# A third set of exponentials, and a head's transposes and output one slot later, evenly spread

## The chip, the cores and the metric

The kernel runs on one core of a Trainium2 chip. The metric is the device time in microseconds (us), the median over several runs; lower is better. The engines that the text speaks of are TensorE (PE; PEld is its weight loads), VectorE (DVE), ScalarE (ACT), GpSimd (POOL), and SyncE (SP), which issues most of the DMAs.

## The reference

Block-causal attention over 8 batches of 8 heads, and a bilinear feed-forward layer on its output, all in float32:

```python
# q, k, v: (8, 8, 576, 64); w_a, w_b: (512, 1536); w_out: (1536, 512)
scores = q @ k.transpose(0, 1, 3, 2) / sqrt(64)
scores = where(pos_q // 64 >= pos_k // 64, scores, -1e9)
attn = exp(scores - max(scores)); attn = attn / (sum(attn) + 1e-9)
x = (attn @ v).transpose(0, 2, 1, 3).reshape(4608, 512)
out = ((x @ w_a) * (x @ w_b)) @ w_out
```

## The kernel before, in words

The 64 heads are worked through in **slots**, one head's scores per slot (the loop at L599). Three generators hold a head's steps, and a table of steps, `SLOT` (L595), says in which order a slot runs them, for which head, and with how many filling matmuls behind each.

- `softmax(i)` (L374), in slot i: on PE the scores, in five groups, named here by their width: the side block (L412, 128 columns) with the last tile `sl` (512, L392), then 256, 320 and 448 columns. Each has its maximum on DVE (L398) and its exponentials on ACT (L401, written into the tiles `e` and `e_s`). The last step comes at the start of slot i+1: row sums and reciprocals on DVE (L435 to L442, `rc`), then POOL multiplies all the tiles of exponentials by them (L445). Score tiles come from a ring of three PSUM banks (`ps_sc`, L262), and a head uses four; the side block and the 320 columns share one.
- `turn(i)` (L450): PE transposes the exponentials in four groups (L468), here T3, T2, T1 and T0 after the tile that they read (T1 has `e_s` as well). Each goes to one of two PSUM buffers called `tp`; ACT rounds it to `ah` (L470) and DVE takes the remainder `al` (L472, in `lower`). `SLOT` runs T3, T2 and T1 of head s-1 late in slot s, and T0 early in slot s+1. `lower` of T1 is issued only with the next step, and those of T1 and T0 are put behind the reciprocals `rc` of the next head (`behind_of`).
- `values(i)` (L484), in slot i+2: the output in two steps, here V1 (four matmuls with `ah`, L517) and V2 (the side block and four with `al`, L521 and L523), into the one PSUM bank `av` and one more `tp` buffer. ACT and DVE add it up into `xf` (L527 to L532); after every second head it is split into `xh` and `xl` and stored.

The exponentials live in `NE` = 2 sets of buffers (L283), taken in turn, so head i+2 writes where head i was read. Heads 0 to 7 (`NATIVE`) run in plain float32, without `al`.

From slot 10.2 on (`MOE_FROM`) PE gets filling work: the feed-forward layer of the batches that are done (`first_pass`, L545, matmuls of 288 columns at L217, called the filling matmuls below). `want` (L583) says how many of them have been issued at a given point of a slot: an even ramp up to 240 at slot 2·8+`LAG`, then 36 to a slot (one for each unit of the third number in `SLOT`). Every second slot also prepares queries and keys of two heads (L337 to L345) and issues the DMAs that spread them (L356 to L359); `split_v` (L361) prepares the values of the head before. Weights are converted meanwhile, mostly on DVE (`convert`, L127). After the last slot come the rest of the first pass and two further passes, whose code the change does not touch.

Each engine's instructions are put into one fixed order when the program is built, and each engine then works in that order. "Head 44 is of batch 5, number 4" is how the names in the built order are read: `tp_2_0` is T0 of number 2 of its batch; the last number of a name is that of the buffer.

Of the kernel before, what the change touches and what calls it, by code (L numbers as in the profile page):

```python
# [26 lines left out]
MOE_FROM = 10.2  # L27
# [4 lines left out]
XQ = lambda nc: nc.scalar  # L32
PE_ORDER = []
NATIVE = 8
SPARE = 8
WARM = 9
KEEP = {(0,3):4,(1,0):2,(1,1):2,(1,2):2,(1,3):6}
# [15 lines left out]
def attention_then_bilinear_ffn(  # L53
# [10 lines left out]
    nc = tc.nc  # L64
    B, H, D, S = kT.shape
# [39 lines left out]
    def f32(ap):  # L105
        return ap.bitcast(F32)

    def split(hi, lo, src, hi_eng, lo_eng):
        if hi_eng is nc.scalar:
            nc.scalar.copy(hi, src)  # L110
        else:
            hi_eng.tensor_copy(hi, src)
        return lo_eng.tensor_tensor(lo, src, f32(hi), op=ALU.subtract)  # L113
# [3 lines left out]
    def behind_of(ins, key):  # L117
        if key in last:
            tc.add_manual_dep(ins.ins, last[key].ins.name, NOSYNC, reason="after work that is waited for")
# [88 lines left out]
    marks = []  # L208
# [71 lines left out]
    W = S - BLK  # L280
    SIDE, SIDE_T = 3, 1
    SC = slice(P * SIDE_T, P * SIDE_T + BLK), slice(P * SIDE_T + BLK, P * (SIDE_T + 1))
    NE = 2  # L283
    e_bufs, s_bufs = [], []
    for i in range(NE):
        es = [const.tile([P, ew[t]], F32, name=f"e{i}_{t}") for t in range(NT)]
# [24 lines left out]
    def load_pair(p):  # L311

        b, h = divmod(2 * p, H)
        n = f"{b}_{h}"
        if 2 * p < NATIVE:
            qp = apool.tile([P, 1, SQ], F32, tag="q2", name=f"qp{n}", bufs=3)
            kp = apool.tile([P, 2, S], F32, tag="k2", name=f"kp{n}", bufs=3)
        else:
            qp = apool.tile([P, 2, SQ], F32, tag="qp", name=f"qp{n}", bufs=1)
            kp = apool.tile([P, 2, S], F32, tag="kp", name=f"kp{n}", bufs=1)  # L320
        nc.sync.dma_start(kp[:, 1], kT[b, h:h + 2].rearrange("h d s -> (h d) s"))
        nc.sync.dma_start(qp[:, 0], qT[b, h:h + 2].rearrange("h d s -> (h d) s"))
        pairs[p] = qp, kp
        for j in range(2):
            heads[2 * p + j] = {"q": qp[j * D:(j + 1) * D, 0], "k": kp[j * D:(j + 1) * D, 1]}

    def load_v(i):
        b, h = divmod(i, H)
        vr = heads[i]["vr"] = apool.tile([P, NCH + 1, D], F32, tag="vr", name=f"vr{b}_{h}", bufs=3)
        nc.sync.dma_start(vr, vm[b, h])  # L330

    def split_q(p):
        qp = pairs[p][0]
        if 2 * p < NATIVE:
            nc.vector.tensor_scalar_mul(qp[:, 0], qp[:, 0], SCALE)
            return
        nc.scalar.mul(qp[:, 1].bitcast(F32R), qp[:, 0], SCALE)  # L337
        behind_of(nc.vector.scalar_tensor_tensor(
            qp[:, 0], qp[:, 0], SCALE, qp[:, 1], op0=ALU.mult, op1=ALU.subtract), "rc")

    def split_k(p):
        kp = pairs[p][1]
        if 2 * p >= NATIVE:
            nc.scalar.copy(kp[:, 0].bitcast(F32R), kp[:, 1])
            nc.gpsimd.tensor_tensor(kp[:, 1], kp[:, 1], kp[:, 0], op=ALU.subtract)  # L345

    def spread(i):

        if i < NATIVE:
            return  # L350
        qp, kp = pairs[i // 2]
        n = "%d_%d" % divmod(i, H)
        own = slice(i % 2 * D, (i % 2 + 1) * D)
        q2 = heads[i]["q2"] = apool.tile([P, SQ], F32R, tag="q2", name=f"q2{n}", bufs=3)
        k2 = heads[i]["k2"] = apool.tile([P, 2, S], F32R, tag="k2", name=f"k2{n}", bufs=3)
        for j in range(2):  # L356
            part_ = slice(j * D, (j + 1) * D)
            nc.sync.dma_start(f32(q2[part_]), qp[own, 1 - j])
            nc.sync.dma_start(f32(k2[part_]), kp[own])  # L359

    def split_v(i):  # L361

        if i < NATIVE:
            return
        n = "%d_%d" % divmod(i, H)
        vr = heads[i]["vr"]
        v2 = heads[i]["v2"] = apool.tile([P, NCH + 1, 2, D], F32R, tag="v2", name=f"v2{n}", bufs=2)
        split(v2[:, :, 0], v2[:, :, 1], vr, nc.scalar, nc.gpsimd)
# [5 lines left out]
    def softmax(i):  # L374

        t, n = heads[i], "%d_%d" % divmod(i, H)
        native = i < NATIVE
        if native:
            qm, ks = t["q"], [t["k"]]
        else:  # L380
            qm, ks = t["q2"], [t["k2"][:, j] for j in range(2)]
        es, e_s = e_bufs[i % NE]

        nm, rc = (apool.tile([P, NT + 1], F32, tag=x, name=f"{x}{n}") for x in ("nm", "rc"))
        sm = s_bufs[i % NE]

# [63 lines left out]
    def turn(i):  # L450

        b, h = divmod(i, H)
        n = f"{b}_{h}"
        es, e_s = e_bufs[i % NE]
        native = i < NATIVE
        ah = apool.tile([P, NCH, W], F32 if native else F32R, tag="ah", name=f"ah{n}")
        al = None if native else apool.tile([P, NCH, W], F32R, tag="al", name=f"al{n}")
        heads[i]["a"] = ah, al
        for t in range(LAST, -1, -1):
            tp = ps_t.tile([P, 4, P], F32, tag="tp", name=f"tp{n}_{t}", bufs=2)  # L460
            m = min(t + 2, NCH)
            todo = [es[t][:, c * P:(c + 1) * P] for c in range(m)]
            if t == SIDE_T:
                assert m == SIDE
                todo.append(e_s)
            m = len(todo)
            for c, src in enumerate(todo):
                mark = nc.tensor.transpose(tp[:, c], src, ident)  # L468
            cols = slice(P * t, P * (t + 1))
            nc.scalar.copy(ah[:, :m, cols], tp[:, :m])  # L470
            def lower(tp=tp, m=m, cols=cols):
                return nc.vector.tensor_tensor(al[:, :m, cols], tp[:, :m], f32(ah[:, :m, cols]), op=ALU.subtract)  # L472

            if t == SIDE_T and not native:
                yield mark
                behind_of(lower(), "rc")
                continue
            if not native:
                ins = lower()
                if t == 0:  # L480
                    behind_of(ins, "rc")
            yield mark

    def values(i):  # L484
# [88 lines left out]
    NH = B * H  # L573
    LAG = 2
    per_slot = 2 * F1 * (2 * 3 * NCC + 3 * NO) // H
    behind = 3 * F1 * NO
# [5 lines left out]

    def want(now):  # L583

        n = (now - H - LAG) * per_slot - behind
        if now < 2 * H + LAG:
            n = (H * per_slot - behind) * (now - MOE_FROM) / (2 * H + LAG - MOE_FROM)
        return int(n)

    keep = None  # L590


    S_, T_, V_ = softmax, turn, values

    SLOT = [(S_, 0, 3), (S_, -1, 0), (T_, -2, 4), (S_, 0, 4), (V_, -2, 3), (S_, 0, 3),  # L595
            (T_, -1, 4), (V_, -2, 3), (S_, 0, 3), (T_, -1, 5), (T_, -1, 4)]
    fill = sum(m for _, _, m in SLOT)
    gens = {}
    for s in range(NH + LAG):  # L599
        p, odd = divmod(s + 4, 2)  # L600
        if p < NH // 2 and not odd:
            load_pair(p)
        if s < NH:
            load_v(s)
        steps = []
        for what, i, m in SLOT:
            i += s
            if 0 <= i < NH:
                steps.append((gens.get((what, i)) or gens.setdefault((what, i), what(i)), m))
        due = k = 0  # L610
        for g, m in steps:
            mark = next(g)
            if not m:
                continue
            for _ in range(KEEP.get((s, k), 0)):
                keep = keep or ps_t.tile([P, W], F32, tag="av", name="keep")
                nc.tensor.matmul(keep, z[:, :P], z, start=True, stop=True)
            marks.append(mark)
            if k == 1 and 0 < s <= NH:
                split_v(s - 1)  # L620
            if k == (3 if odd else 4) and s + 2 < NH:
                if not odd and s:
                    split_q((s + 2) // 2)
                    split_k((s + 2) // 2)
            if k == (3 if odd else 6) and s + 2 < NH:
                spread(s + 2)
            k += 1
            due += m
            now = s + due / fill
            while n_conv < 5 * int(now * CONV_PER_SLOT + CONV0):  # L630
                next(conv, None)
                n_conv += 1
            if now > MOE_FROM and moe is None:
                moe = first_pass()
            while moe and n_moe < want(now):
                next(moe)
                n_moe += 1
# [142 lines left out]
    k = 0  # L780
# [8 lines left out]
    for kp in range(KP):  # L789
        g = sums_x(raw, kp, "0_0")  # L790
# [6 lines left out]
    k = 0  # L797


    for ps_ in range(2):  # L800
        fs = list(range(F1 + ps_ * F2, F1 + (ps_ + 1) * F2))
        for tt in range(NT2):
# [42 lines left out]
            if ps_ == 0 and tt == 0:  # L845
                background(1e4)
                conv = convert_w(parts(range(F1 + F2, NF)), nc.vector, paced=True, stage=stage)
                n_conv, start, k, pace = 0, 0, 0, STEP2
# [45 lines left out]
```

## Time and profile before

| | |
|---|---|
| runs of the kernel before | 1281.93, 1277.46, 1283.12 us; median 1281.93 us |
| the profiled execution | 1281.83 us, of which 1279.8 us lie between its first and last instruction (the span); mean granted PE clock 0.988 |
| busy over the span | PE 97%, PEld 92%, DVE 78%, ACT 53%, POOL 43% |
| attention | slots from 0 to about 640 us of the span |

All times inside the span are read from this one execution, which is within 0.1 us of the median. PE's busy time is no measure of how full it is: its matmuls overlap, and their ends are modelled. A slot's length is therefore read from the start of one head's side block (L412) to that of the next head's.

### The profile page before, as it was taken

To read this page: it belongs to the slowest core of one execution; us is meant where nothing else is said; L and a number is where in the kernel's file an instruction comes from. 1 tells how busy PE (TensorE), PEld (TensorE's weight loads), DVE (VectorE), ACT (ScalarE), POOL (GpSimd) and SP (SyncE) were. 2 spreads that over 40 slices of the span, in tenths; PEclk is the share of its full clock that TensorE was granted. 3 is DMA by queue.
4 is the path that set the end of the run, shared out by engine and by line. 5 is a ranking of instruction groups with operands and counts; after the bars stand their busy time and mean duration, and the time that the engine had idled before them with its cause. 6 is when DMAs were issued, how large, how long until landed. Compare 5 with 4: busy or idle time off the path is not lost.

```text
span 1279.8 us, 23524 instructions
## 1 busy us (share of the span) xinstructions
PE 1239.3 (97%) x7849; PEld 1173.2 (92%) x7849; DVE 999.2 (78%) x2389; ACT 683.6 (53%) x1722; POOL 554.9 (43%) x679
## 2 busy tenths in 40 slices
PE   9988999999999999999988998999999999999998
PEld 5668998999999999999988998999999999999998
DVE  6878887777887877877699999899967577577553
ACT  5788787788787788888745423233222222122210
POOL 4567565566665565665422322223223123123231
PEclk8999999999999999999998999999999999999999
DMA  5467766777767767676225355364466442243131
GB/s 195 132 167 201 187 174 175 178 171 181 170 167 179 179 171 176 167 178 155 87 94 171 100 180 194 139 206 164 141 220 244 145 149 79 70 149 98 52 99 62
DMA packets 93496, 196.58 MB, mean 154 GB/s; under 512 B 11968, under 2 KB 52928, under 8 KB 93376
## 3 DMA queue, kind: packets, MB, share of 16 engines
q1 hardware_dynamic: 88768, 185.64, 51.4%
q10 hardware_dynamic: 4608, 9.44, 2.0%
q8 instruction: 63, 1.03, 0.3%
q14 instruction: 57, 0.47, 0.1%
HBM read 96.47 MB, written 47.19 MB: 112 GB/s over the span
## 4 chain that ended last, share of the span: by engine, by line
PE 71%; DVE 15%; DMA 4%; issue 4%; ACT 3%; POOL 2%; SPq 1%; ACTq 0%; DVEq 0%; POOLq 0%
PE pso_z L754 13%; PE ps L217 12%; PE tp L468 7%; PE psx_z L708 6%; PE psw_z L708 6%; PE psv_z L708 6%; PE pso L217 4%; PE s L392 4%; PE psy_z L708 3%; PE av L517 3%; PE av L523 3%; PE sl L392 2%; DMA kp<-kT 2%; PE av L507 2%; DVE sw L147 1%
## 5 line engine op out<-in xcount | busy, mean ns | idle before, releaser
L113 POOL TENSOR_TENSOR h_z<-u_z,h_z 128x384 fp32r<-128x384 f32 x96 | 112.8, 1175 | 391.4 <-ACT h_z L110 379.8
L217 PE MATMUL ps<-xh,wab 128*128 128x288 f32 x1024 | 241.8, 304 | 1.2 <-ACT a L241 1.2
L754 PE MATMUL pso_z<-h_z,wo 128*128 128x384 f32 x1152 | 204.0, 335 | 4.5 <-POOL h_z L113 4.5
L445 POOL TENSOR_SCALAR e<-e,rc 128x512 f32<-128x512 f32 (+3 forms) x256 | 151.6, 604 | 127.9 <-DVE rc L442 118.1
L754 PEld LDWEIGHTS pso_z<-h_z,wo 128*128 128x128 f32 x1152 | 199.6, 188 | 7.0 <-POOL h_z L113 7.0
L217 PEld LDWEIGHTS ps<-xh,wab 128*128 128x128 f32 x1024 | 172.3, 189 | 4.7 <-ACT a L241 1.4
L472 DVE TENSOR_TENSOR al<-tp,ah 128x512 fp32r<-128x512 f32 x224 | 131.6, 608 | 31.5 <-ACT ah L470 31.0
L217 PE MATMUL ps<-xl,wab 128*128 128x288 f32 x512 | 154.1, 301 | 0.0
L468 PE MATMUL tp<-ident,e 128*128 128x128 f32 x832 | 136.1, 278 | 10.4 <-POOL e L445 4.0
L470 ACT CAST ah<-tp 128x512 fp32r<-128x512 f32 x224 | 116.4, 531 | 50.3 <-PE tp L468 47.5
L110 ACT CAST h_z<-u_z 128x384 fp32r<-128x384 f32 x96 | 49.3, 514 | 167.7 <-DVE u_z L733 160.2
L217 PE MATMUL pso<-hh,wo 128*128 128x288 f32 x512 | 128.1, 311 | 4.3 <-ACT hh L110 4.3
L708 PE MATMUL psx_z<-xh,wab 128*128 128x384 f32 x384 | 118.5, 344 | 7.2 <-DVE u_z L726 6.7
L468 PEld LDWEIGHTS tp<-ident,e 128*128 128x128 f32 x832 | 100.8, 142 | 25.7 <-POOL e L445 9.5
L401 ACT ACTIVATE e<-s,nm 128x192 f32<-128x192 f32 (+2 forms) x192 | 101.5, 529 | 32.4 <-DVE nm L398 23.2
L708 PE MATMUL psw_z<-xh,wab 128*128 128x384 f32 x384 | 117.0, 340 | 0.8 <-DVE u_z L728 0.8
L708 PE MATMUL psv_z<-xh,wab 128*128 128x384 f32 x384 | 116.7, 339 | 0.5 <-DVE u_z L730 0.4
L398 DVE TENSOR_REDUCE nm<-s 128x1 f32<-128x192 f32 (+3 forms) x256 | 109.9, 431 | 2.4
L217 PEld LDWEIGHTS ps<-xl,wab 128*128 128x128 f32 x512 | 96.5, 188 | 3.4
L217 PEld LDWEIGHTS pso<-hh,wo 128*128 128x128 f32 x512 | 88.3, 192 | 6.6 <-ACT hh L110 5.3
L113 POOL TENSOR_TENSOR v<-vr,v 128x320 fp32r<-128x320 f32 x56 | 50.2, 897 | 89.3 <-ACT v L110 67.9
L392 PE MATMUL s<-k,q 128*128 128x256 f32 x336 | 81.2, 322 | 2.2 <-ACT e_s L401 1.9
(142 smaller groups left out, 2919.5 us busy)
## 6 DMA issues: line engine op xcount, KB each, us to landing
k<-kp SPq DMA_DIRECT2D x112, 288.0 KB, 3.8
xr<-xd SPq DMA_DIRECT2D x48, 384.0 KB, 3.5
pt<-part SPq DMA_DIRECT2D x96, 192.0 KB, 3.5
q<-qp SPq DMA_DIRECT2D x112, 160.0 KB, 2.6
raww<-wab SPq DMA_DIRECT2D x24, 512.0 KB, 3.8
qp<-qT SPq DMA_DIRECT2D x32, 320.0 KB, 3.2
vr<-vm SPq DMA_DIRECT2D x64, 160.0 KB, 3.1
kp<-kT SPq DMA_DIRECT2D x32, 288.0 KB, 3.5
```

What stands on the lines that cost most here:

```text
L110: nc.scalar.copy(hi, src)
L113: return lo_eng.tensor_tensor(lo, src, f32(hi), op=ALU.subtract)
L217: mm = nc.tensor.matmul(ps, w_, d_, start=(i == 0), stop=(i == n - 1))
L392: mark = nc.tensor.matmul(ps[:, :w], qm[:, q0[t]:q0[t] + P], kk[:, :w], start=(i == 0), stop=(i == len(ks) - 1))
L398: nc.vector.tensor_reduce(nm[:, t:t + 1], view, axis=AX.X, op=ALU.max, negate=True)
L401: nc.scalar.activation(out, view, AF.Exp, bias=bias, accum_out=sm[:, t, :1])
L445: nc.gpsimd.tensor_scalar(ev, ev, rc[:, t:t + 1], 1.0, op0=ALU.mult, op1=ALU.mult)
L468: mark = nc.tensor.transpose(tp[:, c], src, ident)
L470: nc.scalar.copy(ah[:, :m, cols], tp[:, :m])
L472: return nc.vector.tensor_tensor(al[:, :m, cols], tp[:, :m], f32(ah[:, :m, cols]), op=ALU.subtract)
L708: nc.tensor.matmul(ps, wt[:, i, iw], j[:, ix], start=start and kp == 0 and i == 0 and j is xh, stop=kp == KP - 1 and i == 1, skip_group_ch ...
L754: nc.tensor.matmul(ps, wt[:, a, osl], b, start=i == 0, stop=i == 3 * len(fs) - 1)
```

## The change

The third set: `NE` becomes 3, and the program reserves 1024 bytes of scratch for dynamic DMAs in place of the default. A set takes (256 + 384 + 512 + 512 + 128) columns of 4 bytes and 40 bytes of sums, 7,208 bytes in each partition.

The order: up to slot 9 a table `SLOT1` is used, which is the old one with V2 moved ahead of T3. From slot 10 (`SW`) on, all four transposes of head s-2 stand in slot s, evenly spread, and V1 and V2 of head s-3 between them; the loop has one more slot. `want` counts from 2.85 (`FFLAG`) in place of 2 slots of lag, so the ramp to 240 filling matmuls reaches to slot 18.85. `lower` follows its transposes at once and is no longer put behind `rc`. At slot 10 the values of head 8 are split a second time.

```diff
+SW = 10
+FFLAG = 2.85
...
-    NE = 2
+    NE = 3
...
-            if t == SIDE_T and not native:
-                yield mark
-                behind_of(lower(), "rc")
-                continue
             if not native:
-                ins = lower()
-                if t == 0:
-                    behind_of(ins, "rc")
+                lower()
             yield mark
...
-        n = (now - H - LAG) * per_slot - behind
-        if now < 2 * H + LAG:
-            n = (H * per_slot - behind) * (now - MOE_FROM) / (2 * H + LAG - MOE_FROM)
+        n = (now - H - FFLAG) * per_slot - behind
+        if now < 2 * H + FFLAG:
+            n = (H * per_slot - behind) * (now - MOE_FROM) / (2 * H + FFLAG - MOE_FROM)
...
-    SLOT = [(S_, 0, 3), (S_, -1, 0), (T_, -2, 4), (S_, 0, 4), (V_, -2, 3), (S_, 0, 3),
-            (T_, -1, 4), (V_, -2, 3), (S_, 0, 3), (T_, -1, 5), (T_, -1, 4)]
+    SLOT = [(S_, 0, 3), (S_, -1, 0), (T_, -2, 4), (V_, -3, 3), (S_, 0, 4), (T_, -2, 4), (V_, -3, 3),
+            (S_, 0, 3), (T_, -2, 4), (S_, 0, 4), (T_, -2, 4)]
...
-    for s in range(NH + LAG):
+    for s in range(NH + LAG + 1):
...
-            if k == 1 and 0 < s <= NH:
-                split_v(s - 1)
+            if k == 1 and 0 < s - (s >= SW) <= NH:
+                split_v(s - 1 - (s >= SW))
...
-    nc = bacc.Bacc("TRN2", target_bir_lowering=False, num_devices=1)
+    nc = bacc.Bacc("TRN2", target_bir_lowering=False, num_devices=1, dynamic_dma_scratch_size=1024)
```

What this does to the order, at three places. First PE, between T0 and V1 of head 42 (number 2 of batch 5), in the slot of head 44 before:

```order
L392 MATMUL s_4_6567<-k_4_6313,q_4_6312 128x256 x2
L217 MATMUL ps_4_0_1_6542<-xl_2_0_5834,wab_81 128x288
L217 MATMUL ps_4_0_1_6542<-xh_2_0_5833,wab_81 128x288
L217 MATMUL ps_4_0_1_6542<-xh_3_0_6151,wab_81 128x288
L468 MATMUL tp_2_0_6555<-ident,e_0_107 128x128 x2
L217 MATMUL ps_4_0_1_6542<-xl_3_0_6152,wab_81 128x288
L217 MATMUL ps_4_0_1_6542<-xh_3_0_6151,wab_81 128x288
L217 MATMUL ps_4_0_1_6586<-xh_0_0_5197,wab_81 128x288
L217 MATMUL ps_4_0_1_6586<-xl_0_0_5198,wab_81 128x288
L517 MATMUL av_2_6578<-ah_2_6442,v_2_6399 128x512
```

and now, from T0 of the same head on (line numbers are two higher here):

```order
L470 MATMUL tp_2_0_6593<-ident,e_0_107 128x128 x2
L219 MATMUL ps_4_0_1_6591<-xl_0_0_5267,wab_81 128x288
L219 MATMUL ps_4_0_1_6591<-xh_0_0_5266,wab_81 128x288
L219 MATMUL ps_4_0_1_6591<-xh_1_0_5584,wab_81 128x288
L219 MATMUL ps_4_0_1_6591<-xl_1_0_5585,wab_81 128x288
L414 MATMUL s_5_6608<-k_5_6351,q_5_6350 128x128 x2
L219 MATMUL ps_4_0_1_6591<-xh_1_0_5584,wab_81 128x288
L394 MATMUL sl_5_6607<-k_5_6351,q_5_6350 128x512 x2
L219 MATMUL ps_4_0_1_6591<-xh_2_0_5902,wab_81 128x288
L219 MATMUL ps_4_0_1_6591<-xl_2_0_5903,wab_81 128x288
L470 MATMUL tp_3_3_6634<-ident,e_3_120 128x128 x4
L219 MATMUL ps_4_0_1_6591<-xh_2_0_5902,wab_81 128x288
```

Before, four filling matmuls stood between T0 and V1, which reads what T0 made. Now T0 ends its slot; the next head's side block and `sl` and T3 of head 43 follow, and V1 of head 42 comes after three more filling matmuls.

Second, again PE, what follows on the scores of 320 columns of head 44, before:

```order
L392 MATMUL s_4_6526<-k_4_6313,q_4_6312 128x320 x2
L217 MATMUL ps_4_0_1_6586<-xh_0_0_5197,wab_81 128x288
L217 MATMUL ps_4_0_1_6586<-xh_1_0_5515,wab_81 128x288
L217 MATMUL ps_4_0_1_6586<-xl_1_0_5516,wab_81 128x288
L468 MATMUL tp_3_3_6603<-ident,e_3_120 128x128 x4
L217 MATMUL ps_4_0_1_6586<-xh_1_0_5515,wab_81 128x288
L217 MATMUL ps_4_0_1_6586<-xh_2_0_5833,wab_81 128x288
L217 MATMUL ps_4_0_1_6586<-xl_2_0_5834,wab_81 128x288
L217 MATMUL ps_4_0_1_6586<-xh_2_0_5833,wab_81 128x288
L521 MATMUL av_2_6614<-ah_2_6442,v_2_6399 128x128
L521 MATMUL av_2_6614<-al_2_6443,v_2_6399 128x128
L523 MATMUL av_2_6578<-al_2_6443,v_2_6399 128x256
```

and now:

```order
L394 MATMUL s_4_6447<-k_4_6241,q_4_6240 128x320 x2
L219 MATMUL pso_1_3_6551<-hh_1_0_5752,wo_80 128x288
L219 MATMUL pso_1_3_6551<-hh_1_1_6068,wo_82 128x288
L219 MATMUL pso_1_3_6551<-hl_1_1_6069,wo_82 128x288
L470 MATMUL tp_2_1_6568<-ident,e_1_108 128x128 x3
L470 MATMUL tp_2_1_6568<-ident,e_s 128x128
L219 MATMUL pso_1_3_6551<-hh_1_1_6068,wo_82 128x288
L219 MATMUL pso_1_3_6551<-hh_1_2_6173,wo_84 128x288
L219 MATMUL pso_1_3_6551<-hl_1_2_6174,wo_84 128x288
L219 MATMUL pso_1_3_6551<-hh_1_2_6173,wo_84 128x288
L394 MATMUL s_4_6579<-k_4_6241,q_4_6240 128x448 x2
L219 MATMUL pso_1_3_6551<-hh_1_3_6271,wo_86 128x288
```

Before, T3, V2, the 448 columns, T2 and T1 all came between these scores and the next head's `sl`. Now only T1, the 448 columns and T0 do, with some sixteen filling matmuls in all.

Third, DVE in the same slot, around the reciprocals of head 43, before:

```order
L435 TENSOR_REDUCE rc_3_6362<-sm_124 128x5
L398 TENSOR_REDUCE nm_4_6522<-s_4_6567 128x1
L439 TENSOR_REDUCE rc_3_6362<-sm_124 64x2
L442 RECIPROCAL rc_3_6362<-rc_3_6362 128x5
L472 TENSOR_TENSOR al_2_6443<-tp_2_1_6506,ah_2_6442 128x4x128
L472 TENSOR_TENSOR al_2_6443<-tp_2_0_6555,ah_2_6442 128x2x128
L430 MEMSET s_4_6526 64x64
```

and now:

```order
L437 TENSOR_REDUCE rc_3_6289<-sm_124 128x5
L474 TENSOR_TENSOR al_2_6472<-tp_2_3_6473,ah_2_6471 128x4x128
L441 TENSOR_REDUCE rc_3_6289<-sm_124 64x2
L444 RECIPROCAL rc_3_6289<-rc_3_6289 128x5
L340 SCALAR_TENSOR_TENSOR qp_6_6116<-qp_6_6116 128x640
L432 MEMSET s_4_6499 64x64
L400 TENSOR_REDUCE nm_4_6443<-s_4_6499 128x1
L474 TENSOR_TENSOR al_2_6472<-tp_2_2_6509,ah_2_6471 128x4x128
```

Before, the remainders of T1 and T0 of head 42 stood together behind the reciprocals. Now the remainder of T3 stands between their parts and that of T2 follows the next maximum; those of T1 and T0 come later in the slot, each by itself.

More of the change, by code (lines that the diff above doesn't have):

```diff
@@ L593, in attention_then_bilinear_ffn @@
     S_, T_, V_ = softmax, turn, values
-    SLOT = [(S_, 0, 3), (S_, -1, 0), (T_, -2, 4), (S_, 0, 4), (V_, -2, 3), (S_, 0, 3),
-            (T_, -1, 4), (V_, -2, 3), (S_, 0, 3), (T_, -1, 5), (T_, -1, 4)]
+    SLOT1 = [(S_, 0, 3), (S_, -1, 0), (T_, -2, 4), (S_, 0, 4), (V_, -2, 3), (S_, 0, 3),
+             (V_, -2, 3), (T_, -1, 4), (S_, 0, 3), (T_, -1, 5), (T_, -1, 4)]
+    SLOT = [(S_, 0, 3), (S_, -1, 0), (T_, -2, 4), (V_, -3, 3), (S_, 0, 4), (T_, -2, 4), (V_, -3, 3),
+            (S_, 0, 3), (T_, -2, 4), (S_, 0, 4), (T_, -2, 4)]
     fill = sum(m for _, _, m in SLOT)
     gens = {}
-    for s in range(NH + LAG):
+    for s in range(NH + LAG + 1):
         p, odd = divmod(s + 4, 2)
@@ L605, in attention_then_bilinear_ffn @@
         steps = []
-        for what, i, m in SLOT:
+        for what, i, m in SLOT if s >= SW else SLOT1:
             i += s
@@ L611, in attention_then_bilinear_ffn @@
         for g, m in steps:
-            mark = next(g)
+            mark = next(g, None)
             if not m:
@@ L617, in attention_then_bilinear_ffn @@
                 nc.tensor.matmul(keep, z[:, :P], z, start=True, stop=True)
-            marks.append(mark)
-            if k == 1 and 0 < s <= NH:
-                split_v(s - 1)
+            if mark:
+                marks.append(mark)
+            if k == 1 and 0 < s - (s >= SW) <= NH:
+                split_v(s - 1 - (s >= SW))
             if k == (3 if odd else 4) and s + 2 < NH:
```

## The prediction

> **What bounds the kernel now.** The page comes first, then the busy times by stage:
>
> ```profile
> span 1279.8 us, 23524 instructions
> PE 1239.3 (97%) x7849; PEld 1173.2 (92%) x7849; DVE 999.2 (78%) x2389; ACT 683.6 (53%) x1722; POOL 554.9 (43%) x679
> ```
>
> ```profile
> core 0: us, PE busy (x) PEld busy (x) DVE busy (x) ACT busy (x) POOL busy (x), PEclk, DMA share, GB/s
> 0.00:97.00 97.00, 88.68 (x502) 60.16 (x502) 74.80 (x208) 67.62 (x183) 55.73 (x80) 0.91 0.56 165
> 97.00:175.70 78.70, 74.17 (x519) 68.46 (x518) 68.39 (x204) 63.62 (x177) 51.80 (x71) 1.00 0.71 188
> 175.70:618.10 442.40, 438.72 (x3153) 420.93 (x3152) 348.12 (x1104) 352.64 (x991) 268.73 (x384) 1.00 0.68 170
> ```
>
> The change's steps lie in these three stages and a few us behind them, about half of the 1279.8. PE leads in all three. How many slots a stage holds is counted from the side blocks (L412, two matmuls a head), in the busy times of that line alone:
>
> ```profile
> 97.00:175.70 78.70, 2.77 (x16) 2.63 (x17) 1.00 0.71 188
> 175.70:618.05 442.35, 15.07 (x90) 14.40 (x91) 1.00 0.68 170
> ```
>
> So 8 slots (10 to 17) take 78.7 us, and 45 (18 to 62) take 442.4, 9.83 each. Two slots that follow each other, an odd and an even one, and then the worst slot and two stretches in it:
>
> ```profile
> 208.30:217.90 9.60, 9.60 (x73) 9.37 (x72) 6.93 (x23) 7.42 (x20) 4.18 (x8) 1.00 0.67 172
> 217.90:227.70 9.80, 9.80 (x71) 9.28 (x71) 8.82 (x27) 8.33 (x26) 8.47 (x12) 1.00 0.64 151
> 194.80:208.30 13.50, 11.62 (x73) 10.74 (x72) 8.63 (x26) 9.08 (x26) 7.09 (x10) 0.87 0.65 172
> 198.00:201.40 3.40, 1.75 (x11) 1.28 (x9) 2.67 (x8) 2.39 (x8) 2.48 (x2) 1.00 0.30 101
> 201.40:204.80 3.40, 3.17 (x13) 3.13 (x14) 1.05 (x4) 1.47 (x4) 2.04 (x5) 0.50 0.95 196
> ```
>
> PE has the same work in each. PEld shows it: 9.37 and 9.28 us, whether the slot is 9.6 or 9.8 long; the even one has 0.2 to 0.3 us of holes that busy PE hides. The timeline shows where: first three rows of the even slot, then the odd slot up to the next two side blocks:
>
> ```profile
> 220.17 0.41 PE L468 MATMUL tp<-ident,e 128*128 128x128 f32 x2
> 220.62 0.37 ACT L470 CAST ah<-tp 128x256 fp32r<-128x256 f32 x1 [0.55 <-PE tp L468]
> 221.05 0.74 PEld L517 LDWEIGHTS av<-ah,v 128*128 128x128 f32 x4 [0.16 <-ACT ah L470]
> ```
>
> ```profile
> 208.29 0.33 PE L412 MATMUL s<-k,q 128*128 128x128 f32 x2
> ...
> 209.24 0.38 PE L468 MATMUL tp<-ident,e 128*128 128x128 f32 x2
> ...
> 210.88 0.86 PE L517 MATMUL av<-ah,v 128*128 128x512 f32 x4
> 211.58 0.43 PE L217 MATMUL ps<-xh,wab 128*128 128x288 f32 x2
> ...
> 217.85 0.33 PE L412 MATMUL s<-k,q 128*128 128x128 f32 x2
> ...
> 227.72 0.33 PE L412 MATMUL s<-k,q 128*128 128x128 f32 x2
> ```
>
> In the even slot V1 starts 0.88 us behind T0 and waits for the cast of T0 (220.62 + 0.37 = 220.99). In the odd one 1.64 us lie between and nothing waits. From side block to side block the odd slot takes 217.85 - 208.29 = 9.56 us, the even one 227.72 - 217.85 = 9.87. The waits of PE and of its loads in the 45 slots say the same:
>
> ```profile
> PE tp L468 <- DVE al L472: 1.6, 5, 0.4
> PE tp L468 <- POOL e L445: 1.4, 1, 1.4
> PE s L392 <- ACT e_s L401: 0.5, 1, 0.5
> ```
>
> ```profile
> PEld tp L468 <- POOL xl L113: 3.3, 8, 0.6
> PEld av L517 <- ACT ah L470: 3.3, 20, 0.2
> ```
>
> All but one of these rows are transposes without a free `tp` buffer or finished exponentials, or V1 behind T0.
>
> **Slots 18 to 62 (term A).** By the new order T0 ends its slot, and V1 comes in the next one, behind eleven filling matmuls, the side block, `sl` and T3. A filling matmul takes 0.13 us, by the starts of these:
>
> ```profile
> 617.70 0.29 PE L217 MATMUL pso<-hh,wo 128*128 128x288 f32 x1
> 617.83 0.29 PE L217 MATMUL pso<-hl,wo 128*128 128x288 f32 x1
> ```
>
> So T0 to V1 becomes at least 11 x 0.13 = 1.4 us plus those three, more than the 1.64 us at which the odd slot does not wait. The 0.31 us of an even slot go, 23 x 0.31 = 7.1. POOL's multiplication gets a slot of slack, and T2 and T1, which stood five filling matmuls apart, are spread, so `al` has time to free the buffers. All that could go is 442.4 - 45 x 9.56 = 12.2 us; of the 5.1 beyond the even slots' own loss the slot at 194.8 alone holds 13.5 - 9.87 = 3.6. There POOL came late and T3 waited:
>
> ```profile
> 201.63 1.11 PE L468 MATMUL tp<-ident,e 128*128 128x128 f32 x4 [1.42 <-POOL e L445]
> ```
>
> From 201.4 PE then ran at half clock for 3.4 us, behind 3.4 us in which it was busy for 1.75; with 3.13 us of weight loads in them, some 1.6 us more than at full clock. The Trainium skill (TensorE: Matmul & The Clock Gate, "What's actually happening") lets the clock fall to half after an idle window of about 3.4 us. The trace disagrees, since half of such a window was busy. By that page this wait could not have cost the clock, and the sum would be half of the 1.6 us poorer, 1272.
>
> `lower` behind its transposes puts the remainder of T3 between the parts of `rc` (0.6 us by the row on L472 below); POOL's slot of slack hides that, and without it each head's exponentials would be 0.6 us late. The load of a head's values waits on SP for the split of the head three back, which now stands one slot ahead of that load and not two. Most of a slot is left, so I take 0; if it were used up, the loads of queries and keys queued behind it on SP would start later.
>
> I take the 7.1 and half of the 5.1: A = -9.6, between -12.2 (every slot at 9.56) and 0.
>
> **Slots 10 to 17 (term B).** Here a step of depth is paid: one head's transposes and output are moved out of these slots, and the ramp issues 240 x 7.8 / 8.65 = 216 filling matmuls by slot 18 in place of 240. That work comes later, on a full PE: 24 x 0.13 = 3.2 us, and for one head, from rows of the odd slot,
>
> ```profile
> 212.68 0.60 PE L468 MATMUL tp<-ident,e 128*128 128x128 f32 x4
> 213.03 0.51 PE L217 MATMUL ps<-xh,wab 128*128 128x288 f32 x2
> ...
> 213.51 0.22 PE L521 MATMUL av<-ah,v 128*128 128x128 f32 x1
> ...
> 214.44 0.43 PE L217 MATMUL ps<-xh,wab 128*128 128x288 f32 x2
> ```
>
> V1 0.70, V2 0.93, three groups of transposes of 0.35 and half a one: 2.8. Together 6.0 us. In return these slots shrink. DVE has 68.4 us of work in them, and loses the remainders of one head:
>
> ```profile
> L472 DVE TENSOR_TENSOR al<-tp,ah 128x512 fp32r<-128x512 f32 x224 | 131.6, 608 | 31.5 <-ACT ah L470 31.0
> ```
>
> That is 2.4 us, so 66.0 stay. If DVE never idled the stage would take 66.0 us; at its share of now (87%) 75.9. I take 71, the middle: B = 71 + 6.0 - 78.7 = -1.7, between -6.7 and +3.2. The values of head 8, split once more, run on ACT and POOL beside this and cost nothing; without that cover, under 1 us.
>
> **Slots 0 to 9 (term C).** With V2 ahead of T3, POOL has longer for the exponentials, and a third set frees ACT of waits on transposes. At most this wait goes:
>
> ```profile
> PEld tp L468 <- POOL e L445: 5.1, 6, 1.6
> ```
>
> Against it, T3 comes later in eight slots, by up to one group of 0.35: +2.8. I take 0.
>
> **The end (term D).** No scores follow the last heads, so T0 and V1 of head 63 stand four filling matmuls apart as in an even slot, 0.3 us, and the extra slot has nothing else to hide a late cast. I take +0.5, at most +1.5 (five such places). The feed-forward work left after the loop is the same.
>
> The sum: -9.6 - 1.7 + 0 + 0.5 = -10.8. The profiled execution took 1281.83 us, the median is 1281.93: forecast **1271**.
>
> **The rivals.** *The even slots stay long.* DVE is busy for 8.82 of 9.8 us there; if that, not the order, sets 9.87, the 7.1 stay, and only half of the 5.1 and B go: 1281.8 - 2.5 - 1.7 = 1277.6, no change by what this kernel's measurement can tell apart, 0.5% or 6.4 us. Against it: V1's load names the cast of T0.
>
> *Slower: PE waits for a score bank.* The next head's `sl` needs the bank in which the 320 columns were. By the new order sixteen filling matmuls (2.1 us) lie between them, T1 and T0 (0.5), and the 320, 448 and side columns, twice each: 1,792 columns, by V1's 1,536 in 0.70 us an estimate of 0.8. That makes 3.4 us. Now the way from these scores to the end of their exponentials takes:
>
> ```profile
> 211.98 0.46 PE L392 MATMUL s<-k,q 128*128 128x320 f32 x2
> ...
> 213.85 0.54 ACT L401 ACTIVATE e<-s,nm 128x320 f32<-128x320 f32 x1
> ```
>
> 214.39 - 211.98 = 2.4 us. If queues make it longer than 3.4, PE waits in every slot; 0.35 us over in 53 slots is +18.6, so 1289.6. For it: the order puts a filling matmul between side block and `sl` in odd slots.
>
> *The start changes its clock.* The trace has a granted clock of 0.55 over 15.1 us, which is some 13.6 us at half. One more such stretch costs up to 6.8: 1278; one less: 1264.
>
> ```profile
> 19.70:34.80 15.10, 15.10 (x61) 9.94 (x60) 9.72 (x26) 9.09 (x26) 9.70 (x10) 0.55 0.34 108
> ```
>
> *The smaller scratch slows DMAs, or the gain is none for another reason*: 1282 or more. The queue that carries nearly all of the kernel's data is this one:
>
> ```profile
> q1 hardware_dynamic: 88768, 185.64, 51.4%
> ```
>
> The Trainium skill (SBUF — State Buffer, "SBUF size: 192, 224, or 256?") calls this scratch the ring for descriptors that software makes; no run here shows what it is for.
>
> **How the numbers follow.** Forecast 0.66, with a range of its own of 1265 to 1277; even slots stay 0.15; score bank 0.08; clock 0.04 each way; the last 0.03 and what is not named the same way. Below 1275.5 is faster: most of the forecast (0.58), the better clock and a little of the others, 0.65. Above 1288.3 is slower: the score bank, 0.08. The rest, 0.27, is the same. The range of 1263 to 1281 takes in A at its best with B in the middle and the rival of long even slots; it leaves out the score bank, and B or C at their ends.
>
> **What would show it.** Right: even and odd slots both near 9.6 us, no load of V1 that waits for a cast, none of T waiting for POOL; slots 10 to 17 near 71 us, later slots at 9.6. Wrong: a wait of `sl` for ACT; even slots still at 9.8; slots 10 to 17 at 76 or more; a second long half-clock stretch.

## The result, and the profile after

| | before | after |
|---|---|---|
| runs side by side, median | 1279.37 us (6 runs) | 1296.12 us (6 runs) |
| ratio | | 1.0109, 95% interval 1.0082 to 1.0136 |
| profiled execution / span | 1281.83 / 1279.8 us | 1296.83 / 1294.6 us |
| mean granted PE clock | 0.988 | 0.985 |

The change made the kernel slower by about 1.1% (the two medians alone, divided, give 1.3%); the forecast was 1271 us. The page of after, the row of busy times:

```profile
PE 1240.5 (96%) x7849; PEld 1179.1 (91%) x7849; DVE 998.1 (77%) x2389; ACT 688.3 (53%) x1723; POOL 567.0 (44%) x684
```

PE has the same 7849 matmuls and nearly the same busy time as before (1239.3); what is new is time in which it waits. The busy times by stage say where. The stages are cut, as in the prediction, at the side blocks (L414 now) of heads 10, 18 and 63:

```profile
0.00:98.60 98.60, 88.91 (x502) 61.74 (x502) 76.12 (x213) 68.96 (x187) 58.25 (x84) 0.90 0.58 172
98.60:172.70 74.10, 68.05 (x473) 63.94 (x471) 60.55 (x191) 57.67 (x164) 48.11 (x69) 0.98 0.69 181
172.70:626.30 453.60, 437.89 (x3145) 420.58 (x3144) 350.42 (x1104) 356.51 (x990) 270.14 (x383) 1.00 0.63 167
626.30:1294.60 668.30, 645.65 (x3737) 632.89 (x3735) 511.06 (x884) 205.18 (x384) 190.52 (x150) 0.99 0.42 136
```

Against before that is 98.6 - 97.0 = +1.6 for slots 0 to 9, 74.1 - 78.7 = -4.6 for slots 10 to 17, 453.6 - 442.4 = **+11.2** for slots 18 to 62, and 668.3 - 661.7 = +6.6 from head 63 to the end: +14.8 in all. The third stage was forecast 9.6 us shorter. Its waits, in us, times and the longest:

```profile
ACT qp L339 <- DMA qp<-qT: 24.8, 22, 2.8
PEld sl L394 <- ACT e L403: 16.1, 22, 1.7
PE sl L394 <- ACT e L403: 12.5, 18, 1.5
PEld av L513 <- ACT ah L472: 1.9, 2, 1.7
```

V1 (L513 now) waits for T0's cast in two slots, where before it did in twenty: nearly gone, as forecast. But `sl` now waits for exponentials, that is for its score bank, and ACT waits 24.8 us for loads of queries in 22 places, where before it waited 0.3 us in two. The two belong together. The timeline at the end of an odd slot, whose exponentials of 320 columns free the bank for the `sl` at the start of the even one:

```profile
210.81 0.34 SPq L324 DMA_DIRECT2D qp<-qT  x1
211.12 0.45 PE L394 MATMUL s<-k,q 128*128 128x320 f32 x2
213.82 0.74 ACT L339 ACTIVATE qp<-qp 128x640 fp32r<-128x640 f32 x1 [1.40 <-DMA qp<-qT]
214.58 0.59 ACT L472 CAST ah<-tp 128x512 fp32r<-128x512 f32 x1
215.06 0.53 ACT L403 ACTIVATE e<-s,nm 128x320 f32<-128x320 f32 x1
215.74 0.74 PE L394 MATMUL sl<-k,q 128*128 128x512 f32 x2 [0.94 <-ACT e L403]
```

The load of the next pair's queries is issued at 210.81 and has landed at 213.8. ACT stands in front of its rounding (L339) for 1.40 us; behind it in ACT's order are the cast of T1 and then the exponentials of 320 columns, which end at 215.59, 4.5 us after the scores started. PE, for which the order leaves 3.4 us by the prediction's count, waits 0.94. Before, the same rounding stood behind those exponentials:

```profile
211.70 0.33 SPq L322 DMA_DIRECT2D qp<-qT  x1
213.85 0.54 ACT L401 ACTIVATE e<-s,nm 128x320 f32<-128x320 f32 x1
214.93 0.74 ACT L337 ACTIVATE qp<-qp 128x640 fp32r<-128x640 f32 x1 [0.17 <-DMA qp<-qT]
```

No line of the diff moves this rounding. The built orders of ACT differ all the same: each engine's order is made anew when the program is built, and the steps around have moved. By what rule the build places this instruction, no run here shows. These are ACT's orders in the slot of head 45, before, then after; the numbers count ACT's instructions, and dots stand for what is left out:

```
760 L401 ACTIVATE e_1_118,sm_124<-s_5_6681,nm_5_6677 128x320
...
762 L337 ACTIVATE qp_0_6516<-qp_0_6516 128x640
```

```
756 L339 ACTIVATE qp_0_6437<-qp_0_6437 128x640
757 L472 CAST ah_3_6632<-tp_3_1_6719 128x4x128
758 L403 ACTIVATE e_1_108,sm_114<-s_5_6608,nm_5_6604 128x320
759 L346 CAST kp_0_6438<-kp_0_6438 128x576
...
761 L472 CAST ah_3_6632<-tp_3_0_6743 128x2x128
762 L403 ACTIVATE e_2_109,sm_114<-s_5_6730,nm_5_6604 128x448
```

The rows from 759 on matter later: the rounding of the keys (L346) stands ahead of T0's cast and of the exponentials of 448 columns.

Pair by pair, PE's wait is ACT's wait for the load less a constant. Two more pairs of after, one with a long wait and one with a short one:

```profile
495.65 0.74 ACT L339 ACTIVATE qp<-qp 128x640 fp32r<-128x640 f32 x1 [1.90 <-DMA qp<-qT]
497.57 0.74 PE L394 MATMUL sl<-k,q 128*128 128x512 f32 x2 [1.44 <-ACT e L403]
...
595.74 0.74 ACT L339 ACTIVATE qp<-qp 128x640 fp32r<-128x640 f32 x1 [0.25 <-DMA qp<-qT]
597.77 0.68 PE L394 MATMUL sl<-k,q 128*128 128x512 f32 x2
```

1.90 - 1.44 and 1.40 - 0.94 are both 0.46; and a wait of 0.25 costs nothing. In 17 of the 18 pairs of this stage in which the matmuls of `sl` start late the difference is 0.45 to 0.51 us (in the other one 0.67). The longest wait, 2.82 us in slot 18, is no such pair: there it comes early in an even slot, and V1 waits instead.

### The profile page after: what moved, and what is told of

Its sections match the earlier page's. It is cut to its first block, busy times and chain, and to the rows that moved or that the text cites. A ratio compares the mean times of both kernels' runs of the same rounds, so it can differ in the third digit from the quotient of the medians.

```text
span 1294.6 us, 23327 instructions
## 1 busy us (share of the span) xinstructions
PE 1240.5 (96%) x7849; PEld 1179.1 (91%) x7849; DVE 998.1 (77%) x2389; ACT 688.3 (53%) x1723; POOL 567.0 (44%) x684
## 3 DMA queue, kind: packets, MB, share of 16 engines
q1 hardware_dynamic: 88768, 185.64, 49.6%
## 4 chain that ended last, share of the span: by engine, by line
PE 44%; DVE 17%; DMA 11%; issue 5%; ACT 4%; POOL 4%; SPq 1%; DVEq 0%; ACTq 0%; POOLq 0%
PE pso_z L754 14%; PE psx_z L708 6%; PE psw_z L708 6%; PE psv_z L708 5%; DMA q<-qp 4%; PE pso L219 3%; DMA qp<-qT 3%; PE psy_z L708 3%; PE ps L219 2%; DMA k<-kp 2%; DMA kp<-kT 2%; POOL e L447 2%; PE tp L470 2%; DVE nm L400 2%; DVE al L474 1%
## 5 line engine op out<-in xcount | busy, mean ns | idle before, releaser
L447 POOL TENSOR_SCALAR e<-e,rc 128x512 f32<-128x512 f32 (+3 forms) x256 | 170.0, 676 | 175.0 <-DVE rc L444 162.5
L754 PE MATMUL pso_z<-h_z,wo 128*128 128x384 f32 x1152 | 207.4, 339 | 7.1 <-POOL h_z L115 7.1
L754 PEld LDWEIGHTS pso_z<-h_z,wo 128*128 128x128 f32 x1152 | 202.5, 190 | 10.1 <-POOL h_z L115 9.9
L474 DVE TENSOR_TENSOR al<-tp,ah 128x512 fp32r<-128x512 f32 x224 | 138.5, 619 | 87.5 <-ACT ah L472 86.9
L219 PE MATMUL ps<-xl,wab 128*128 128x288 f32 x512 | 157.8, 308 | 1.4 <-POOL xl L115 1.4
L219 PE MATMUL pso<-hh,wo 128*128 128x288 f32 x512 | 122.6, 307 | 2.2 <-ACT hh L112 2.2
L400 DVE TENSOR_REDUCE nm<-s 128x1 f32<-128x128 f32 (+3 forms) x256 | 110.2, 433 | 4.6
L219 PE MATMUL pso<-hl,wo 128*128 128x288 f32 x256 | 79.5, 310 | 2.1 <-POOL hl L115 2.1
```

The source lines that it names most:

```text
L219: mm = nc.tensor.matmul(ps, w_, d_, start=(i == 0), stop=(i == n - 1))
L400: nc.vector.tensor_reduce(nm[:, t:t + 1], view, axis=AX.X, op=ALU.max, negate=True)
L447: nc.gpsimd.tensor_scalar(ev, ev, rc[:, t:t + 1], 1.0, op0=ALU.mult, op1=ALU.mult)
L754: nc.tensor.matmul(ps, wt[:, a, osl], b, start=i == 0, stop=i == 3 * len(fs) - 1)
```

## The experiments

The theory from the trace: the place of the queries' rounding, with its wait for a load, holds the bank of `sl`. The rivals: the wait is only one of several that the new order makes, and another takes its place; or the later order itself, its third set or its evenly spread steps cost the time. Ratios are to the kernel before, run on the same chip. Stage times are those of slots 18 to 62, 442.4 before and 453.6 after.

**The third set and the scratch alone, in the kernel before.**

```diff
-    NE = 2
+    NE = 3
...
+dynamic_dma_scratch_size=1024
```

> The kernel before with the third set of exponentials and the smaller scratch alone. Theory 1: neither carries any of the loss, 1279 as before, within 3 us. Rival (the smaller scratch or the set's place slows DMAs, by which the queries come late): 1285 or more, with ACT waiting for the query load as in the changed kernel (28.2 us there).

Measured: 1278.98 us, ratio 0.9999 (0.9976 to 1.0023). These two parts carry nothing by themselves. The Trainium skill (SBUF — State Buffer, "SBUF size: 192, 224, or 256?") calls the scratch a ring for descriptors that software makes. The trace agrees so far as it goes: the queue that carries 185.64 MB is named hardware_dynamic, and the smaller scratch costs nothing that this run can tell.

The later order itself needs the third set. In `SLOT` the side block and `sl` of head s, with their exponentials, stand ahead of T3 to T0 of head s-2; with two sets both heads use the same one, so these transposes would read exponentials of the wrong head. A run of the version with the rounding behind (below) on two sets was expected above 1320 us, or at 1274 if a set came free in time. It took 1311.48 us and computes wrong values, so its time answers neither.

**Scores of 320 columns ahead of V2, in after.**

```diff
-... (T_, -2, 4), (V_, -3, 3), (S_, 0, 3), ...
+... (T_, -2, 4), (S_, 0, 3), (V_, -3, 3), ...
```

> The changed kernel with one step moved: the scores of 320 columns stand ahead of V2 and not behind it. Theory 1 (PE waits for the score bank of the 320 columns, because sl now follows them too soon): V2 and three filling matmuls, some 1.3 us, come between, so the 18.0 us that the load of sl waited for ACT fall below 3, slots 18 to 62 go from 453.6 to below 438, and the time from 1296 to about 1280. Rival (the slots are long since ACT and DVE are full, and the bank is only where it shows): the wait moves to another score or to the transposes, and the time stays above 1291.

Measured: 1295.67 us, ratio 1.0135 (1.0102 to 1.0167), stage 451.0. The waits of that stage:

```profile
PEld av L513 <- ACT ah L472: 14.4, 22, 0.8
ACT qp L339 <- DMA qp<-qT: 2.0, 6, 0.6
PEld tp L470 <- POOL e L447: 6.8, 12, 0.9
```

`sl` does not wait any more, and nothing is won: V1 now waits for T0's cast. ACT's order moved here too, by the build alone: the rounding of the queries now stands behind the exponentials of 320 columns in all 22 pairs, and ACT waits only 2.0 us for its loads, while the rounding of the keys still stands ahead of the exponentials of 448 columns. So `sl` may have lost its wait by either move; this run does not tell them apart. The timeline shows how V1's wait comes:

```profile
420.33 0.68 DVE L528 TENSOR_TENSOR xf<-av,avlo 64x512 f32<-64x512 f32 x1
422.12 0.60 DVE L400 TENSOR_REDUCE nm<-s 128x1 f32<-128x448 f32 x1
422.76 0.64 ACT L403 ACTIVATE e<-s,nm 128x448 f32<-128x448 f32 x1
423.38 0.85 ACT L472 CAST ah<-tp 128x256 fp32r<-128x256 f32 x2
423.80 0.98 PE L513 MATMUL av<-ah,v 128*128 128x512 f32 x4 [0.20 <-ACT ah L472]
```

With V2 later, DVE adds up the output ahead of the maximum of the 448 columns; ACT has their exponentials ahead of T0's cast; V1 is last in the queue. So the rival's time held, and other waits took the place of this one.

**The old order, one slot later, not spread.**

```diff
+    SLOT = [(S_, 0, 3), (S_, -1, 0), (T_, -3, 4), (S_, 0, 4), (V_, -3, 3), (S_, 0, 3),
+            (T_, -2, 4), (V_, -3, 3), (S_, 0, 3), (T_, -2, 5), (T_, -2, 4)]
```

> The changed kernel with the old order inside a slot: transposes and output of a head come a slot later, on three sets, but T3, V2, T2 and T1 stand where they stood, with the 320 columns early in the slot. Theory 1: no wait of sl; the even slots keep V1 right behind T0; what is left of the loss is the deeper pipeline (6.0 us of work moved behind the last head, less what slots 10 to 17 gain), so 1280 to 1285. Rival (the extra slot of depth is the loss): about 1296, as the changed kernel.

Measured: 1306.55 us, ratio 1.022 (1.0181 to 1.0258), stage 464.9: worse than either said, by other waits.

```profile
PE tp L470 <- DVE al L474: 17.1, 16, 2.5
PEld tp L470 <- POOL kp L347: 15.2, 10, 2.7
```

Transposes wait for a `tp` buffer that DVE still reads, and for POOL, which is busy with the remainder of the keys. Undoing the even spread wins nothing here; that the spread itself does no harm, the fast versions below show.

**The queries' rounding behind the exponentials of 320 columns, in after.** A dependency that costs no semaphore fixes the order; `last["e1"]` is the last such exponential.

```diff
-        nc.scalar.mul(qp[:, 1].bitcast(F32R), qp[:, 0], SCALE)
+        behind_of(nc.scalar.mul(qp[:, 1].bitcast(F32R), qp[:, 0], SCALE), "e1")
```

> The changed kernel with one ACT instruction moved: the rounding of the queries, which waits for their load, is put behind the exponentials of the 320 columns, on ACT alone; no wait is taken away. Theory 1a (the bank is late since this instruction holds ACT up ahead of those exponentials): the wait of sl for ACT falls from 18.0 to below 5 us and the time to about 1284. Theory 1b (the 320 columns stand too close to sl by themselves): at least 10 us of it stay, and the time stays above 1290.

Measured: **1273.73 us, ratio 0.9962 (0.9946 to 0.9979)**, 0.4% faster than before and 22 us faster than after; it beat even the number of theory 1a. The stage:

```profile
169.40:605.10 435.70, 431.65 (x3145) 418.47 (x3144) 350.10 (x1104) 357.30 (x990) 266.89 (x383) 1.00 0.68 173
```

453.6 - 435.7 = 17.9 us come from here, and the loads of `sl` wait for exponentials 0.8 us in all. The edit names one instruction, but the build moved a second. The rounding of the keys (L346) now stands behind the exponentials of 448 columns, in all 22 pairs:

```profile
421.86 0.73 ACT L339 ACTIVATE qp<-qp 128x640 fp32r<-128x640 f32 x1
...
423.03 0.66 ACT L403 ACTIVATE e<-s,nm 128x448 f32<-128x448 f32 x1
...
423.65 0.69 ACT L346 CAST kp<-kp 128x576 fp32r<-128x576 f32 x1
```

**The same rounding put ahead of those exponentials in the kernel before**, from slot 9 on (it is issued in the odd slot before, and the exponentials are tied behind it).

```diff
+            if t == 1:
+                behind_of(ins, "qp")
...
+                if odd and s >= 9 and s + 3 < NH:
+                    split_q((s + 3) // 2)
```

> The kernel before, with the rounding of the queries put directly ahead of the exponentials of 320 columns on ScalarE from slot 9 on, where it stood behind them. Theory (the new order of TensorE made the distance short, 3.4 us from these scores to sl, where the old order left about 5.8): the same delay on ScalarE is hidden in the old order, sl does not wait, and the time is 1278 to 1283 us. Rival (what stands ahead on ScalarE costs in any order, because T1's and T0's casts and V1 come late too): 22 slots at 0.5 us or more, 1290 us or above.

Measured: 1304.38 us, ratio 1.0208 (1.0164 to 1.0252), stage 460.6. My expectation fell. Two pairs in the timeline, without and with a wait, and the even slots that follow or hold them:

```profile
218.36 0.74 ACT L337 ACTIVATE qp<-qp 128x640 fp32r<-128x640 f32 x1
...
300.00 0.74 ACT L337 ACTIVATE qp<-qp 128x640 fp32r<-128x640 f32 x1 [3.78 <-DMA qp<-qT]
300.77 0.82 DVE L338 SCALAR_TENSOR_TENSOR qp<-qp 128x640 f32<-128x640 f32 x1 [3.73 <-ACT qp L337]
301.43 0.73 PE L392 MATMUL sl<-k,q 128*128 128x512 f32 x2 [1.36 <-ACT e L401]
```

```profile
222.13:231.97 9.84, 9.84 (x73) 9.33 (x71) 8.13 (x26) 8.24 (x26) 7.92 (x12) 1.00 0.58 144
299.74:314.40 14.66, 11.78 (x73) 10.76 (x71) 10.38 (x31) 12.11 (x33) 8.77 (x12) 0.88 0.43 108
```

Where the load is there in time the place costs nothing (9.84 us is an even slot of before). Where it is 3.78 us late, ACT and DVE both stand still and the slot takes 14.66. So it is the wait for the load that costs, in the old order too. It need not cost through `sl`: at 382.49 us a wait of 2.11 us leaves `sl` without one, and the even slot behind it still takes 11.47, since filling matmuls and a transpose wait in its place. The edit moved more than the one rounding (the build placed the keys' differently too), and slots 10 to 17 grew by 7.8 us as well; how the 25 us divide is not shown.

**Two buffers for the loaded queries, in after.**

```diff
-            qp = apool.tile([P, 2, SQ], F32, tag="qp", name=f"qp{n}", bufs=1)
+            qp = apool.tile([P, 2, SQ], F32, tag="qp", name=f"qp{n}", bufs=2)
```

> The changed kernel with a second buffer for a pair's loaded queries, so that the load need not wait until the pair before has been spread. The order of ScalarE stays: the rounding of the queries (0.74 us), the cast of T1, then the exponentials of 320 columns. Theory (it is the load that the rounding waits for which holds the exponentials): in the changed kernel this wait was 28.2 us in 23 slots, 1.2 us each; without it the way from the scores of 320 columns to the end of their exponentials falls from the 4.4 us of the late ones to about 3.2, under the 3.4 that the order leaves, sl no longer waits, and the time is 1274 to 1279 us. Rival (the place in the order is enough, with or without the load): the 0.74 us and the cast still stand ahead, sl keeps waiting some 0.5 us in every other slot, and the time stays at 1285 us or more.

Measured: 1292.82 us, ratio 1.0104 (1.0066 to 1.0143), stage 449.2. The rival's time, but not for its reason; the waits show that the edit did not remove what it was to remove:

```profile
ACT qp L339 <- DMA qp<-qT: 17.7, 21, 1.8
PEld sl L394 <- ACT e L403: 11.4, 22, 1.4
```

With a second buffer the build took loads and rounding a pair earlier together, so the rounding still stood right behind its load. This one tells the two apart only so far as both waits fell together, 24.8 to 17.7 and 16.1 to 11.4.

**Two buffers, with the rounding kept at its pair**, behind T2's cast of the odd slot.

```diff
+            if t == 2:
+                last["before"], last["t2"] = last.get("t2", ins), ins
...
+        behind_of(nc.scalar.mul(qp[:, 1].bitcast(F32R), qp[:, 0], SCALE), "before")
```

> The changed kernel with two buffers for a pair's loaded queries, and the rounding tied to the place behind T2's cast of the odd slot, so that it uses queries loaded a pair earlier (in the two-buffer run before this one ScalarE's order took the rounding a pair earlier too, and it went on waiting for its load). The rounding still stands ahead of the exponentials of 320 columns. Theory (the load's landing is the cost: in the changed kernel the loss of sl is the wait for the load less 0.3 us, pair by pair): no wait of the rounding for a load, sl does not wait, even slots of 9.6 to 9.7 us in place of 10.4, and 1273 to 1279 us. Rival (the 0.74 us of the rounding ahead of the exponentials is enough): sl goes on waiting in even slots, 1285 us or more.

Measured: 1293.27 us, ratio 1.0117 (1.0095 to 1.014), stage 447.7. No rounding of queries waits for a load and `sl` hardly waits, as the theory said; the time, though, stayed, within 3 us of after, since other waits are left:

```profile
PEld tp L470 <- POOL e L447: 9.1, 12, 1.3
PEld sl L394 <- ACT e L403: 2.1, 8, 0.3
```

Followed back from one of them:

```profile
234.84 0.68 ACT L346 CAST kp<-kp 128x576 fp32r<-128x576 f32 x1 [0.46 <-DMA kp<-kT]
235.71 0.38 ACT L472 CAST ah<-tp 128x256 fp32r<-128x256 f32 x1
236.12 0.42 DVE L476 TENSOR_TENSOR al<-tp,ah 128x256 fp32r<-128x256 f32 x1 [1.01 <-ACT ah L472]
238.96 0.18 DVE L444 RECIPROCAL rc<-rc 128x5 f32<-128x5 f32 x1
239.24 1.78 POOL L447 TENSOR_SCALAR e<-e,rc 128x512 f32<-128x512 f32 x2 [2.22 <-DVE rc L444]
242.38 0.52 PE L470 MATMUL tp<-ident,e 128*128 128x128 f32 x3 [0.68 <-POOL e L447]
```

The keys' rounding waits for its own load; T0's cast is behind it, T0's remainder on DVE behind that, then the reciprocals, POOL's multiplication, and T1 late in the even slot waits. In the version that gained 22 us the keys' rounding had moved as well. The next two runs take the two apart.

**The keys' rounding alone behind the exponentials of 448 columns, in after; and the same together with the queries loaded ahead.**

```diff
-            nc.scalar.copy(kp[:, 0].bitcast(F32R), kp[:, 1])
+            behind_of(nc.scalar.copy(kp[:, 0].bitcast(F32R), kp[:, 1]), "e2")
```

> The changed kernel with the rounding of the keys put behind the exponentials of 448 columns on ScalarE; the rounding of the queries stays ahead of those of 320 columns. The version that gained 22 us had, by its order, moved both: with the queries' rounding the keys' fell behind the 448 columns by itself. Theory (the wait for the load of the queries is the larger part): sl loses its wait less 0.3 us in every even slot as before, some 17 us in all, so the time is 1286 to 1294 us. Rival (the keys' rounding, which holds the exponentials of 448 columns and with them the sums, GpSimd's multiplication and T3, is the larger part): 1274 to 1280 us.

> The version with queries loaded a pair ahead (no wait for the load, rounding still ahead of the exponentials of 320 columns), and the rounding of the keys behind the exponentials of 448 columns. Theory (two prices, one for the load of the queries and one for the keys' rounding; neither is left): T3 no longer waits for GpSimd, even slots near 9.6 us, 1274 to 1280 us. Rival (what stands ahead of the exponentials of 320 columns costs even without a wait, 0.74 us a pair): 1288 us or more.

Measured: 1298.44 us, ratio 1.0132 (1.0088 to 1.0175) for the keys alone, with `sl` still waiting (the first row below; the profiled execution, 1293.89 us, is the fastest of its four); 1275.75 us, ratio **0.9965 (0.9946 to 0.9983)**, for both, with the stage in the second:

```profile
PEld sl L394 <- ACT e L403: 8.7, 14, 1.2
```

```profile
172.50:604.90 432.40, 430.37 (x3145) 419.40 (x3145) 355.89 (x1106) 357.38 (x989) 268.62 (x383) 1.00 0.67 174
194.66:204.17 9.51, 9.51 (x72) 9.27 (x71) 7.69 (x25) 7.68 (x22) 6.25 (x9) 1.00 0.65 170
204.17:213.74 9.57, 9.57 (x73) 9.34 (x71) 7.48 (x25) 7.99 (x23) 4.93 (x8) 1.00 0.74 207
```

| slots 18 to 62, us | keys' rounding ahead | keys' rounding behind |
|---|---|---|
| queries' rounding waits for its load | 453.6 (after) | 449.2 |
| it does not wait | 447.7 | 432.4 (loaded ahead), 435.7 (rounding behind) |

So the theory was half of it, and "two prices" that add, as I then wrote, was wrong as well. In these single executions each, taken away alone, saves 4 to 6 us of the 21.2, and both together save all of it. In the medians neither alone saves anything that is clear of the spread: 1293.27 and 1298.44 us against 1296.12. The run with the 320 columns ahead of V2 says the same from another side: queries' rounding behind, keys' rounding ahead, stage 451.0.

A likely reading is that while PE waits at one of the places, the engines catch up for the other: after has one wait of a transpose for POOL (1.3 us), the version with the queries loaded ahead has twelve (9.1). This is argued, not shown, and it is not the whole, since ten such waits (4.7 us) are left with the keys' rounding behind and the queries' still ahead.

**The ramp alone, in the kernel before, and a steeper ramp (`FFLAG` 2.5 in place of 2.85) in the version with the rounding behind.**

```diff
-        n = (now - H - LAG) * per_slot - behind
+        n = (now - H - FFLAG) * per_slot - behind
...
```

> The kernel before, with only the flatter ramp: 216 filling matmuls by slot 18 in place of 240. Theory (term B of the prediction: work moved out of slots 10 to 17 comes back at full price on a full TensorE, 24 x 0.13 = 3.2 us, and the ramp does not give it back in the old order, since its waits are not for the matmuls): +3 us, about 1282. Rival (slots 10 to 17 shrink by the same 3.2 us): no change, 1279.

> The version with the query rounding behind the exponentials of 320 columns, with 2.5 in place of 2.85 slots of lag in the ramp of the filling matmuls: 240 x 7.8 / 8.3 = 226 of them by slot 18 in place of 216. Theory (slots 10 to 17 have idle TensorE time to take them, and what is done there is missing behind head 63): 10 x 0.13 = 1.3 us less, 1272.4 us against 1273.7. Rival (they lengthen the ramp as much as they shorten the end): no change, 1273.7.

Measured: 1279.70 us, ratio 1.0001 (0.9979 to 1.0022), for the ramp alone; 1281.22 us, ratio 1.0009 (0.9986 to 1.0032), for the steeper one, which is 7.5 us worse than the version that it was made from. The ramp alone has 71 - 67 = 4 us more filling work behind head 63 (busy times of the filling matmuls there, before and then with the ramp), yet that stage took 661.9 us against 661.7, and slots 10 to 17 took 76.3 against 78.7:

```profile
618.10:1279.80 661.70, 66.59 (x446) 62.02 (x444) 0.99 0.42 137
```

```profile
614.20:1276.10 661.90, 70.87 (x477) 66.98 (x475) 0.99 0.42 137
```

And the steeper one makes filling matmuls wait for the output that they read, which now comes a slot later. The waits stand in slots 18, 26, 34, 42, 50 and 58, one in each batch, and the last five of these slots take 10.6 to 11.3 us:

```profile
PEld ps L219 <- ACT xh L112: 3.9, 6, 1.2
PEld ps L219 <- POOL xl L115: 3.2, 6, 0.6
```

So the flatter ramp suits the change's later output, and by itself it is nearly free. (The build moved the keys' rounding ahead again in 13 of 22 pairs of the steeper run; even slots that have this and no such wait are mostly 9.5 to 9.7 us long, which speaks against this as the main cause.)

## Why the prediction was wrong

| part | forecast | after | both roundings out of the way: queries loaded ahead | the same: queries' rounding behind |
|---|---|---|---|---|
| C, slots 0 to 9 | 0 | +1.6 | +1.8 | +0.7 |
| B, slots 10 to 17 | -7.7 | -4.6 | -5.0 | -7.0 |
| A, slots 18 to 62 | -9.6 | **+11.2** | -10.0 | -6.7 |
| behind head 63 (deferred work and D) | +6.5 | +6.6 | +8.9 | +8.4 |
| sum | -10.8 | +14.8 | -4.3 | -4.6 |

- **The step that failed is the price of the rival "PE waits for a score bank"**, and with it term A, which put this wait at nothing. The place, the 3.4 us that the order leaves (3.5 by the median of the version with queries loaded ahead), and "a wait of `sl` for ACT" as the sign were right. The way from the scores to the end of their exponentials, 2.4 us, was taken from the trace of before, as if ACT's order were to stay. It did not: the rounding of the queries, with its wait for a load, came to stand inside that way, which then took 4.5 us in the slot shown, and the stage took 453.6 us where 432.8 was forecast. The rival got a chance of 0.08; the built order of ACT at this place, which the prediction does not weigh, spoke for it.
- The rival's price was also put as every slot by 0.35 us. It was every second slot, by the load's wait less 0.46 us; PE's share of these waits is 12.5 us; the 21.2 us between this stage and its best version need the keys' rounding too, which the prediction did not name at all.
- **The mechanism of term A was right, its size only roughly**: with both roundings out of the way the stage is 432.4 or 435.7 us, against 442.4 - 9.6 = 432.8. In the faster of the two the even slots have a median of 9.53 us and the odd ones of 9.55, where before had 9.86 and 9.54: 23 x 0.33 = 7.6 us, near the 7.1 of the even slots. That the whole sum came out so near is partly luck, since half of the other 5.1 was a guess. There the wait of V1 behind T0 is gone, as said, and transposes wait for DVE or POOL in one place each.
- **Term B**: 74.1, 73.7 and 71.7 us in place of the 71 taken midway between two bounds. The middle was not reasoned, so where it is met, that is luck. Of the deferred 6.0 us the 3.2 of the ramp (24 x 0.13 is 3.1, to be exact) cost nothing alone: with the ramp alone PE is busy for 640.2 us in place of 637.7 behind head 63, and the stage is no longer; 24 of its 661.7 us had been idle. What else lengthens that stage, by 6.3 to 9.6 us in the versions with this ramp and the later output, one head's transposes and output (2.8) and the last slot among it, is not settled; with only the third set it was 2 us longer as well, so some of this is not the order's.
- **Term C**: not told from nothing. Two builds whose first slots are the same reach head 10 at different times (below).
- Even with the failed step mended the gain is 4 to 5 us, not 10.8: the stage behind head 63 and the start give back a part, and A or B is short by 3 us.
- The rival of long even slots is refuted by the 9.53; the one that the smaller scratch slows DMAs by the run with it alone, 0.9999.

## What to carry to other kernels

When a change rearranges one engine's steps, read the built order of every engine on the new chain, not only of the one that is rearranged: a chain timed in the old trace holds only as long as nothing has moved into it. An instruction that waits for a load does not belong in front of work that frees a buffer for the bounding engine; pin it behind, or load earlier. And when a cure for one wait brings nothing, look for a second one that was covered by it before giving up the theory: two that cover each other show their price only when both are gone.

## What the runs showed of the hardware

- The load of a pair's queries (320 KB) took 2.9 us from issue to landing in the median of after. ACT's wait for it passed on to `sl` on PE one for one beyond a slack of some 0.46 us: 1.40 gave 0.94, 1.90 gave 1.44.
- The start differs, and its granted clock with it, between profiled executions whose first slots are the same: head 10 came at 97.0 us with a granted clock of 0.91 in the kernel before, and with the ramp alone at 95.1 us with 0.93. So a difference of some 2 us there need not be the effect of an edit.
